# Keys transposed in blocks on VectorE, wider products for values and wo: 1186 TensorE instructions instead of 2224

## The chip, the core and the metric

The kernel runs on one core of a Trainium2 chip. The core has TensorE (matrix products into PSUM), VectorE, ScalarE and GpSimd (elementwise work), and SyncE, which here issues nearly all transfers. All transfers run over 16 DMA engines. In the profile the engines are called PE (PEld for its weight loads), DVE, ACT, POOL and SP. The metric is the device time of one execution in microseconds (us), the median of several runs.

## What is computed

A decode step for one token: an attention block and a gated feed-forward block side by side, both fed by the same layer norm of `x`, and their sum added to `x`. All data are float32.

```python
xn = _layernorm(x)                                # x: 1 x 1 x 1024
# attention: 32 query heads, 4 key/value heads of 128, last W = 4096 of 65536 positions
q = xn @ wq                                       # 1024 x 4096
k, v = k_cache[:, :, Sk - W:, :], v_cache[:, :, Sk - W:, :]   # each repeated for 8 query heads
p = softmax(q . k * Dh ** -0.5)
attention = (p @ v).reshape(1, 1, 4096) @ wo      # 4096 x 1024
# feed-forward
h = gelu_tanh(xn @ w_gate) * (xn @ w_up)          # each 1024 x 3584
out = x + attention + h @ w_down                  # 3584 x 1024
```

Each weight and each key and value of the window is used once: 94.4 MB are read and 4 KB written.

## The kernel before

**Stream.** One tile, `ring` (128 partitions x 32768 floats), holds whatever is being read. The list `PLAN` gives the loads in order, each with its column and the load whose place it takes: wq in two halves (q0, q1), then keys and values of heads 0 and 1 (k0, v0), w_gate's first half (g0), keys and values of heads 2 and 3 (k1, v1), w_gate's second half (g1), w_up's first half in two quarters (ua, ub) and its second half (u1), wo in two halves (o0, o1), a small piece of w_down (m), and w_down in three parts (d0, d1, d2). After a load has been worked on, `used` issues the loads that take its place, on SyncE's queue in that order. So o0 waits for the last reader of ua and ub, o1 for u1, d0 for o0, d1 and d2 for o1.

**Order.** The loop at lines 774 to 824 walks `PLAN` and emits the work on each load. Every engine does its instructions in the order in which they are emitted. The class `Flow` notes which tile columns each instruction touches and, in a second pass, puts in the waits between engines and for transfers; PSUM is tracked by whole banks. Nearly every instruction goes through one helper, so the profile puts them all on line 225, and tiles tell them apart.

**Projections** (`project`, lines 468 to 482). A load of wq, w_gate or w_up holds four rows per partition (the input index is 512 jj + 4 p + r). Rows r = 0 and 2 go to TensorE: `xz` holds the normalized input in one column of 32 zeroed ones, and the 512-wide blocks of the weights run through four 32-column strips of the array into the PSUM tile `acc`. Rows 1 and 3 go to VectorE, which adds weight times input into the SBUF tile `part`; `projected` then sums `part` over the partitions on TensorE into the same `acc`.

**Attention.** `transpose_keys` (511 to 522) turns a head's 4096 x 128 keys with 32 TensorE transposes into PSUM and copies them out in eight 512-wide pieces on ScalarE and VectorE; `scores` runs the queries against each piece, and VectorE takes maxima; `exponentials` are ScalarE's. `transpose_probs` turns the probabilities through TensorE; `values` (563 to 575) multiplies each 32-partition strip with its own 128 columns of values. After the values of heads 2 and 3, `maxima` (582 to 590) is emitted, with its VectorE part, ahead of the work on g1; `factors` and `normalizers` follow later, and `heads` scales the outputs after ub.

**Feed-forward.** `gelu` and `gated` work on `acc` for w_gate and w_up as 128 x 512 and 96 x 512. `hidden` (664 to 698) brings the hidden vector onto the partitions with 32 small TensorE products and copies into `hz`.

**Output.** `outputs` splits wo's 32 rows per partition: even ones go to TensorE, `accumulate` with four 256-wide products each, odd ones to VectorE into `out_part`. `downs` does the same for w_down; the last pieces of d2 are narrow, so that little work is left behind the last transfer. Of d2, 32 pieces of 3 KB are loaded as ten small transfers into `moved` instead, which changes how many bytes each of the 16 DMA engines gets.

Of the kernel before, what the change touches and what calls it, by code (L numbers as in the profile page):

```python
# [25 lines left out]
DOWN = (16, 8, 4)  # L26
PIECES = ((0, 16), (0, 4, 8), (0, 2, 3, 4))
KEPT = (1, 3, 5, 7, 9, 11)
EPS = 1e-5
# [5 lines left out]
MC = 768  # L35
MOVED = ((0, 0, 0, 12, 4), (0, 1, 12, 12, 4), (1, 0, 24, 5, 1), (1, 1, 29, 3, 1))
SIZES = {"tp": NB, "acc": 2 * NB, "part": 8 * NB, "rows": 2 * NB}
# [16 lines left out]
class Flow:  # L54
# [4 lines left out]
    def __init__(self, nc, plan=None):  # L59
# [3 lines left out]
        self.touched = {}  # L63
        self.sems = {}
# [44 lines left out]
    def note(self, k, ins):  # L109
# [3 lines left out]
        for access, writes in [(a, False) for a in ins.ins] + [(a, True) for a in ins.outs]:  # L113
# [22 lines left out]
            self.touched[name] = kept  # L136
        self.ops.append((engine, dma, needs))
# [128 lines left out]
def decode_layer(nc, x, k_cache, v_cache, wq, wo, w_gate, w_up, w_down, out):  # L266
# [16 lines left out]
    def source(kind, i):  # L283
# [11 lines left out]
        return grouped(w_down, P * sum(DOWN[:i]), DOWN[i])  # L295
# [4 lines left out]
    def load(key, at):  # L300
# [18 lines left out]
        if key == ("d", 2):  # L319
            end = 2 * n - MC  # L320
            nc.gpsimd.memset(loaded[key][:, end:2 * n], 0.0)
            both = src[:, 0:2].rearrange("p t n -> p (t n)")
            nc.sync.dma_start(loaded[key][0:P:2, :2 * n], both[0:P:2])
            nc.sync.dma_start(loaded[key][1:P:4, :2 * n], both[1:P:4])
            nc.sync.dma_start(loaded[key][3:P:4, :end], both[3:P:4, :end])
            pieces = pieces[1:]
# [4 lines left out]

    moved = consts.tile([P, 2, MC], F32, name="moved")
    moved_h = consts.tile([P, 2], F32, name="moved_h")

    def load_moved():


        rest = w_down[DF - 4 * P:, D - MC:].rearrange("(r x) n -> x r n", x=16)[13]
        for s, a, first, count, step in MOVED:
            for j in range(step):  # L340
                to = 32 * a + j
                nc.sync.dma_start(
                    moved[to:to + 4 * (count // step):4, s], rest[first + j:first + count:step]
                )
# [8 lines left out]
    x_rows = work.tile([NJ, NR * P], F32, name="x_rows")  # L353
# [3 lines left out]
    x_out = work.tile([P, CO], F32, name="x_out")  # L357
    nc.vector.memset(x_out, 0.0)
# [6 lines left out]
    ident = consts.tile([P, P], F32, name="ident")  # L365
    nc.gpsimd.memset(ident, 0.0)
# [7 lines left out]
    xz = consts.tile([P, NR, NJ, 32], F32, name="xz")  # L374
    nc.vector.memset(xz, 0.0)
    qz = consts.tile([P, 2, 32], F32, name="qz")
    nc.vector.memset(qz, 0.0)

    hz = consts.tile([P, TD + 1, 32], F32, name="hz")
    nc.vector.memset(hz, 0.0)  # L380
    nc.gpsimd.memset(moved, 0.0)
    nc.gpsimd.memset(moved_h, 0.0)
    oz = consts.tile([P, HQ + 1, 32], F32, name="oz")
    nc.vector.memset(oz, 0.0)
    units = consts.tile([P, 2, 32], F32, name="units")
    nc.vector.memset(units, 0.0)
    nc.vector.memset(units[:, 0, 31:32], 1.0)
    unit = units.rearrange("p t m -> p (t m)")[:, 31:63]

    same = consts.tile([P, 4, 32], F32, name="same")  # L390
    nc.vector.tensor_add(same[:, 0, :], ident[:, 0:32], ident[:, 32:64])
    nc.vector.tensor_add(same[:, 1, :], ident[:, 64:96], ident[:, 96:128])
# [20 lines left out]
    def layer_norm():  # L413
        xt_p = small("xt_p")
        for r in range(NR):
# [29 lines left out]
            xz[:, :, :, 0], xc.rearrange("p (r j) -> p r j", r=NR), st[:, 7:8], None, op0=ALU.mult  # L445
# [14 lines left out]
    def blocks(kind, z, w, count, start, stop):  # L460
        for n in range(count):
            b, c = divmod(n, 4)
            nc.tensor.matmul(
                acc[kind][32 * c:32 * c + 32, b, :], z, w[:, n * NB:(n + 1) * NB],
                start=start, stop=stop,
            )

    def project(kind, jj, w, rows, count):
        n = count * NB
        for k, r in enumerate(rows):  # L470
            first = jj == 0 and r < 2
            if first and r == 0:
                acc[kind] = psum.tile([P, 2, NB], F32, name="acc_" + kind, tag="acc")
                part[kind] = work.tile([P, 8 * NB], F32, name="part", tag="part")
# [6 lines left out]
    def projected(kind, count):  # L481
        blocks(kind, unit, part[kind], count, False, True)
# [6 lines left out]
    def queries(q_sb):  # L489
        q_p = psum.tile([P, 2, 4, 4], F32, name="q_p", tag="tp", bufs=2)  # L490
        for b in range(2):
            for hh in range(4):
                nc.tensor.matmul(
                    q_p[:, b, hh, :], q_sb[:, b, hh * P:(hh + 1) * P], ident[:, 0:P:32],
                    start=True, stop=True,
                )
            nc.vector.tensor_copy(
                qz[:, b, 0:16].rearrange("p (s t h) -> p s t h", s=2, t=2),
                q_p[:, b].rearrange("p h (s t) -> p s t h", s=2),
            )  # L500
# [10 lines left out]
    def transpose_keys(g, kn, steps, vector):  # L511
        if g not in keys:
            keys[g] = work.tile([P, 8, NB], F32, name="kT")
# [260 lines left out]
    for key, _, _ in PLAN:  # L774
# [33 lines left out]
        elif kind in ("ua", "ub", "u"):  # L808
# [4 lines left out]
            elif kind == "ub":  # L813
                heads()
# [36 lines left out]
```

## Time and profile before

| | |
|---|---|
| time, median of 3 runs | 226.21 us (226.15 to 226.31) |
| profiled execution, first to last instruction | 224.8 us |
| TensorE matmuls busy | 126.0 us, 1107 instructions, and as many weight loads |
| VectorE busy | 112.1 us |
| ScalarE busy | 28.2 us |
| GpSimd busy | 2.8 us |
| read from memory | 94.38 MB, 420 GB/s over the span |
| instruction packets on queue 8 | 8, 0.13 MB |

The span is the time from the first to the last instruction of one profiled execution; that execution has no other time of its own, and the runs' median lies 1.4 us above the span. A row of the timeline reads: start, duration, engine, line, operation, output tile <- input tiles, shape, how many instructions were merged, and in brackets the idle time before it and what ended that. A transfer appears with the engine that issued it (SPq), and the row shows the issue, not the transfer; when it has landed can be read from the first instruction that waited for it.

### The profile page before, as it was taken

Reading aid. Unit: us, or ns where it says so; the run is one execution under the profiler, and the core shown is the slowest. Engines: PE = TensorE matmul, PEld = TensorE weight load, DVE = VectorE, ACT = ScalarE, POOL = GpSimd, SP = SyncE. Lnnn points to the kernel's source line nnn. Section 1 sums busy time; section 2 is a strip of 40 time slices with the busy share of each in tenths; the row PEclk is TensorE's granted clock in tenths of the full one; section 3 lists DMA queues with packets and bytes.
Section 4 is the critical chain, followed back from the end, with each engine's and each line's share of the span. In section 5 each row is a group of like instructions: output and inputs, shape, how many; then the busy total and the mean of one; then the engine's idle time right before and its main releaser. Section 6 shows DMA issues by size and latency. Waiting matters only on the chain.

```text
span 224.8 us, 2511 instructions
## 1 busy us (share of the span) xinstructions
PE 126.0 (56%) x1107; PEld 65.6 (29%) x1107; DVE 112.1 (50%) x142; ACT 28.2 (13%) x54; POOL 2.8 (1%) x9
## 2 busy tenths in 40 slices
PE   0120910539899891999836751237308988900976
PEld 0010200104634731755601110001003887400442
DVE  7030920591333282336039489339708932992942
ACT  2030000002415600454400220000000000000000
POOL 3000000000000000000000000000000000010000
PEclk9999975596969999799988795557965855665699
DMA  9889889799997999999989999999989989999994
GB/s 374 374 385 548 373 373 560 338 408 464 439 490 338 429 443 452 391 488 408 472 355 449 434 449 429 490 399 420 469 385 455 467 385 461 434 397 394 426 407 172
DMA packets 3194, 94.53 MB, mean 421 GB/s; under 512 B 446, under 2 KB 718, under 8 KB 1040
## 3 DMA queue, kind: packets, MB, share of 16 engines
q1 hardware_dynamic: 3160, 94.38, 97.8%
q8 instruction: 8, 0.13, 0.2%
q14 instruction: 2, 0.02, 0.0%
q10 hardware_dynamic: 24, 0.01, 0.0%
HBM read 94.38 MB, written 0.00 MB: 420 GB/s over the span
## 4 chain that ended last, share of the span: by engine, by line
DMA 67%; DVE 20%; PE 10%; SPq 1%; ACT 1%; issue 1%; POOL 0%; DVEq 0%
DMA ring<-in_B_w_gate 26%; DMA ring<-in_A_wq 18%; DMA ring<-in_A_wo 13%; DVE part L225 13%; DMA ring<-in_B_w_down 10%; PE tp L225 6%; PE out L225 3%; DVE out_part L225 3%; DVE rows L225 2%; SPq L225 1%; PE acc L225 1%; DVE g_sb L225 1%; ACT kT L225 1%; DVE hz L225 1%; DVE kT L225 0%
## 5 line engine op out<-in xcount | busy, mean ns | idle before, releaser
L225 PE MATMUL acc<-ring,xz 128*32 128x512 f32 x176 | 32.2, 808 | 37.3 <-DMA ring<-in_A_wq 22.2
L225 DVE SCALAR_TENSOR_TENSOR part<-ring,xz,part 128x3584 f32<-128x3584 f32 (+1 forms) x9 | 37.2, 4129 | 22.0 <-DMA ring<-in_A_wq 12.5
L225 PE MATMUL tp<-ident,ring 128*128 128x128 f32 x128 | 21.0, 309 | 7.1 <-DMA ring<-in_A_k_cache 5.0
L225 PEld LDWEIGHTS acc<-ring,xz 128*32 128x32 f32 x176 | 7.2, 139 | 58.2 <-issue 26.7
L225 DVE SCALAR_TENSOR_TENSOR out_part<-ring,oz,out_part 128x1024 f32<-128x1024 f32 x16 | 20.6, 1285 | 0.6
L225 PEld LDWEIGHTS tp<-ident,ring 128*128 128x128 f32 x128 | 15.4, 154 | 16.7 <-DMA ring<-in_A_k_cache 5.9
L225 PE MATMUL out<-ring,hz 128*32 128x256 f32 x168 | 12.1, 438 | 13.5 <-DMA ring<-in_B_w_down 13.4
L225 DVE COPY kT<-tp 128x512 f32<-128x512 f32 x12 | 8.1, 690 | 19.1 <-PE tp L225 19.1
L225 PE MATMUL out<-ring,oz 128*32 128x256 f32 x120 | 12.0, 586 | 9.6 <-DMA ring<-in_A_wo 9.6
L225 ACT ACTIVATE kT<-tp 128x512 f32<-128x512 f32 x20 | 11.5, 596 | 26.6 <-PE tp L225 26.6
L225 PE MATMUL tp<-ident,kT 128*128 128x4 f32 (+4 forms) x64 | 13.4, 343 | 1.6 <-DVE hz L225 1.6
L225 PEld LDWEIGHTS tp<-ident,kT 128*128 128x128 f32 (+2 forms) x64 | 13.1, 294 | 2.2 <-DVE hz L225 1.8
L225 PE MATMUL acc<-part,units 128*32 128x512 f32 x44 | 8.1, 817 | 8.7 <-DVE part L225 8.7
L225 DVE TENSOR_SCALAR part<-ring,xz 128x3584 f32<-128x3584 f32 (+1 forms) x3 | 6.5, 2171 | 12.3 <-DMA ring<-in_A_wq 7.5
L225 PEld LDWEIGHTS out<-ring,hz 128*32 128x32 f32 x168 | 5.6, 125 | 20.0 <-DMA ring<-in_B_w_down 15.8
L225 PEld LDWEIGHTS out<-ring,oz 128*32 128x32 f32 x120 | 5.7, 166 | 16.0 <-DMA ring<-in_A_wo 10.6
L225 DVE SCALAR_TENSOR_TENSOR out_part<-ring,hz,out_part 128x1024 f32<-128x1024 f32 x6 | 7.7, 1285 | 4.9 <-DMA ring<-in_B_w_down 4.7
L225 PE MATMUL s<-kT,qz 128*32 128x512 f32 x64 | 9.3, 709 | 0.0
L225 DVE TENSOR_REDUCE m<-s 128x2 f32<-128x1024 f32 x4 | 4.9, 1225 | 7.7 <-PE s L225 7.7
L225 PE MATMUL o<-ring,pT 128*32 128x128 f32 x256 | 7.8, 274 | 1.0 <-ACT pT L225 1.0
L225 PEld LDWEIGHTS o<-ring,pT 128*32 128x32 f32 x256 | 6.7, 110 | 1.9 <-ACT pT L225 1.9
L225 PE MATMUL tp<-ident,x_rows 2*128 2x2 f32 x4 | 0.6, 253 | 10.4 <-DMA x_rows<-in_A_x 10.4
(96 smaller groups left out, 73.3 us busy)
## 6 DMA issues: line engine op xcount, KB each, us to landing
ring<-in_B_w_gate SPq DMA_DIRECT2D x2, 7168.0 KB, 29.5
ring<-in_A_k_cache SPq DMA_DIRECT2D x4, 2048.0 KB, 19.0
ring<-in_A_v_cache SPq DMA_DIRECT2D x2, 4096.0 KB, 26.1
ring<-in_B_w_up SPq DMA_DIRECT2D x2, 3584.0 KB, 22.3
ring<-in_B_w_up SPq DMA_DIRECT2D x1, 7168.0 KB, 25.8
ring<-in_B_w_down SPq DMA_DIRECT2D x2, 2048.0 KB, 20.7
ring<-in_B_w_down SPq DMA_DIRECT2D x2, 512.0 KB, 21.1
ring<-in_B_w_down SPq DMA_DIRECT2D x2, 256.0 KB, 21.2
```

Of the source, the lines that this page charges most:

```text
L225: return lambda *a, **k: self.flow.issue(self.engine, lambda: call(*a, **k))
```

## The change

Loads, their order and their places in `ring` stay the same, but for w_down's tail.

- **Keys.** `turn_keys` transposes a head's keys where they lie, in 32 x 32 blocks, with one VectorE instruction of 128 x 4096. `spread_keys` then copies the sixteen (partition group, block column) combinations, 32 partitions x 1024 elements each, to their places in a second tile: four on GpSimd, seven on VectorE, five on ScalarE. The tile has two buffers. The work is emitted as turn, spread, turn (next head), scores, spread (next head), exponentials, scores.
- **Values.** Two strips at a time: 64 partitions x 256 columns, half of which `heads` uses, so that `heads` has eight scaled additions instead of four.
- **Projections.** The dictionary `VECTOR` says which rows go to VectorE: six of wq's eight, five of w_gate's, seven of w_up's (before, four of each). TensorE's blocks of w_gate and w_up are 512 and 384 wide, eight of them.
- **GELU** is fused into three VectorE instructions per half. `hidden` transposes with two VectorE instructions.
- **wo and w_down.** `accumulate_halves` takes a row in two 512-wide products, alternately on the lower and the upper two strips; `add_halves` adds its four sums into `out_part`. Three more rows of wo go to VectorE.
- **Tail of w_down.** Every fourth partition's first three rows of d2 (12 KB each, 32 of them, with one dummy row before them whose factor is zero) are left out of d2 and loaded into `moved` by three transfers of eleven rows.
- Zeroed tiles become one tile and one memset; a few constants are added; GpSimd's instructions wait for the one before.

```diff
+LONG, SHORT = 16, 12
+WIDTHS = (NB, P // 4 * SHORT)
+WO_KEPT = ((14,), (2, 6, 14))
+PAIRED = 18
+VECTOR = {
+    ("q", 0): (0, 1, 2, 3), ("q", 1): (1, 3), ("g", 0): (1, 2, 3), ("g", 1): (1, 3),
+    ("u", 0): (0, 1, 2, 3), ("u", 1): (1, 2, 3),
+}
...
+OWN = 11
+AWAY = 3
...
+        if engine == ENG.Pool and not dma:
+            needs.update(self.pool)
+            self.pool = [k]
...
         if key == ("d", 2):
...
+            nc.gpsimd.memset(loaded[key][:, :AWAY * n], 0.0)
+            for t, end in zip(pieces, pieces[1:3]):
+                part_of = src[:, t:end].rearrange("p t n -> p (t n)")
+                for some in (slice(0, P, 2), slice(1, P, 4)):
+                    nc.sync.dma_start(loaded[key][some, t * n:end * n], part_of[some])
+            pieces = pieces[2:]
...
+        moved.append(work.tile([P, AWAY, D], F32, name="moved", tag="part"))
+        there = moved[0][:32 + 4 * OWN].rearrange("p t n -> p (t n)")
+        nc.gpsimd.memset(there, 0.0)
...
+        for j in range(3):
+            nc.sync.dma_start(
+                there[32 + j:32 + 4 * OWN:4],
+                rest[OWN * j:OWN * j + OWN, at * D:(at + AWAY) * D],
+            )
...
-            if r % 2 == 0:
-                blocks(kind, xz[:, r, jj, :], wr, count, first, False)
+            if r not in VECTOR[kind, jj]:
...
+                blocks(kind, xz[:, r, jj, :], wr, first, False)
             else:
-                add_scaled(part[kind][:, :n], wr, xz[:, r, jj, 0:1], first)
...
+                add_scaled(part[kind][:, :n], wr, xz[:, r, jj, 31:32], first)
...
-    def transpose_keys(g, kn, steps, vector):
...
+    def turn_keys(kn):
+        nc.vector.transpose(kn, kn)
+
+    def spread_keys(g, kn):
+        keys[g] = work.tile([P, 8, NB], F32, name="kT", bufs=2)
+        kT = keys[g].rearrange("p i n -> p (i n)").rearrange("p (j a k) -> p j a k", a=4, k=32)
+        kn = kn.rearrange("p (j b k) -> p j b k", b=4, k=32)
+        for n in range(16):
+            a, b = n % 4, (n + n // 4) % 4
+            to, of = kT[32 * b:32 * b + 32, :, a], kn[32 * a:32 * a + 32, :, b]
+            if a == b:
+                nc.gpsimd.tensor_copy(to, of)
+            elif n % 2 or n == 4:
+                nc.vector.tensor_copy(to, of)
             else:
-                nc.scalar.activation(keys[g][:, i, :], t_p, AF.Copy)
+                nc.scalar.activation(to, of, AF.Copy)
...
-                for c in range(4):
-                    j = 16 * b + 4 * c + jj
+                for c in (0, 2):
                     nc.tensor.matmul(
-                        o_p[32 * c:32 * c + 32, g, :], pT[:, b, jj, 32 * c:32 * c + 32],
-                        vn[:, j * DH:(j + 1) * DH],
-                        start=(b == 0 and jj == 0), stop=(b == 1 and jj == 3),
+                        o_p[32 * c:32 * c + 64, g], pT[:, b, jj, 32 * c:32 * c + 64],
+                        vn[:, b, c:c + 2, jj], start=(b == 0 and jj == 0), stop=(b == 1 and jj == 3),
                     )
...
         for g in range(2):
...
+            for n in range(4):
+                f, t = divmod(n, 2)
+                add_scaled(
+                    o_sb[:, g, :], o_p[:, 2 * g + f, t], weights[:, g, f, t:t + 1], n == 0
+                )
...
+        for b, n in enumerate(WIDTHS):
+            gs, ts, hs = g_sb[:, b, :n], t_sb[:, b, :n], h_sb[:, b, :n]
+            nc.scalar.activation(gs, acc["g"][:, b, :n], AF.Copy)
+            nc.vector.scalar_tensor_tensor(ts, gs, 0.044715, gs, op0=ALU.mult, op1=ALU.mult)
+            nc.vector.scalar_tensor_tensor(ts, ts, 1.0, gs, op0=ALU.add, op1=ALU.mult)
             nc.scalar.activation(hs, ts, AF.Tanh, scale=GELU_C)
+            nc.vector.scalar_tensor_tensor(gs, hs, 1.0, gs, op0=ALU.add, op1=ALU.mult)
...
+        t = 0
+        for b, count in enumerate((LONG, SHORT)):
+            rows = h_sb[:, b, :32 * count].rearrange("p (k t) -> p t k", t=count)
+            nc.vector.transpose(hz[:, t:t + count, :], rows)
+            t += count
...
+    def accumulate_halves(z, w, stop=False):
...
+        a = len(halves) % 2
+        for b in range(2):
+            c = 2 * a + b
+            nc.tensor.matmul(
+                half_p[32 * c:32 * c + 32], z, w[:, b * NB:(b + 1) * NB],
+                start=len(halves) < 2, stop=stop,
+            )
+        halves.append(a)
+
+    def add_halves():
+        for c in range(4):
+            r, cols = slice(32 * c, 32 * c + 32), slice(c % 2 * NB, c % 2 * NB + NB)
+            nc.vector.tensor_add(out_part[r, cols], out_part[r, cols], half_p[r])
...
-            transpose_keys(2 * i, kn[:, :half], range(8), (1, 4, 6))
+            turn_keys(kn[:, :half])
             if i == 0:
                 queries(q_sb)
+            spread_keys(2 * i, kn[:, :half])
+            turn_keys(kn[:, half:])
             s = scores(2 * i)
-            transpose_keys(2 * i + 1, kn[:, half:], range(4), ())
+            spread_keys(2 * i + 1, kn[:, half:])
             exponentials(2 * i, s)
-            transpose_keys(2 * i + 1, kn[:, half:], range(4, 8), (4, 5, 7))
             s = scores(2 * i + 1)
```

More of the change, by code (lines that the diff above doesn't have):

```diff
@@ L356, in decode_layer @@
         nc.scalar.dma_start(x_rows[j:j + 1, :], x_in[j:j + 1, :])
-    x_out = work.tile([P, CO], F32, name="x_out")
-    nc.vector.memset(x_out, 0.0)
+    sizes = (CO, NR * NJ * 32, 2 * 32, (TD + 1) * 32, (HQ + 1) * 32, 2 * 32)
+    zeros = consts.tile([P, sum(sizes)], F32, name="zeros")
+    nc.vector.memset(zeros, 0.0)
+    ends = [sum(sizes[:k]) for k in range(len(sizes) + 1)]
+    x_out, xz, qz, hz, oz, units = (zeros[:, a:b] for a, b in zip(ends, ends[1:]))
+    xz = xz.rearrange("p (r j m) -> p r j m", j=NJ, m=32)
+    qz, hz, oz, units = (z.rearrange("p (t m) -> p t m", m=32) for z in (qz, hz, oz, units))
     x_in = x.rearrange("a b (h c n) -> (a b c) h n", h=2, c=4)
@@ L588, in maxima @@
         )
-        for c in range(1, 4):
-            nc.vector.tensor_copy(top[:, c, :], top[:, 0, :])
+        nc.vector.tensor_copy(top[:, 1:4, :], top[:, 0:1, :].to_broadcast([2, 3, 32]))
     def factors():
@@ L653, in gelu @@
             nc.scalar.activation(hs, ts, AF.Tanh, scale=GELU_C)
-            nc.vector.tensor_scalar(hs, hs, 0.5, 0.5, op0=ALU.mult, op1=ALU.add)
-            nc.vector.tensor_mul(gs, gs, hs)
+            nc.vector.scalar_tensor_tensor(gs, hs, 1.0, gs, op0=ALU.add, op1=ALU.mult)
     def gated():
-        for b in range(2):
-            n = rows[b]
-            h = copies[b][:n]
-            g, u = (a.unsqueeze(1).to_broadcast(h.shape) for a in (g_sb[:n, b], acc["u"][:n, b]))
-            nc.vector.tensor_mul(h, g, u)
@@ L694, in hidden @@
[L694 to L702 removed]
+                h_p[r, :AWAY], where[:, 4 * a:4 * b], hz[:, t:t + AWAY, 31], start=True, stop=True
+            )
+            nc.vector.tensor_copy(moved_h[r], h_p[r, :AWAY])
@@ L736, in downs @@
         tiles = [loaded["d", i][:, n * D:(n + 1) * D] for i in range(3) for n in range(DOWN[i])]
[L737 to L738 removed]
+        n = 32 + 4 * OWN
+        for s in range(AWAY):
+            add_scaled(out_part[:n], moved[0][:n, s], moved_h[:n, s:s + 1], False)
         for t in KEPT:
```

210 lines of the change are left out of this document (81 added, 129 removed).

## The prediction

> **What bounds the kernel now.** I read the busy shares first, then the queues, then the chain that ended last.
>
> ```profile
> span 224.8 us, 2511 instructions
> PE 126.0 (56%) x1107; PEld 65.6 (29%) x1107; DVE 112.1 (50%) x142; ACT 28.2 (13%) x54; POOL 2.8 (1%) x9
> q1 hardware_dynamic: 3160, 94.38, 97.8%
> q8 instruction: 8, 0.13, 0.2%
> DMA 67%; DVE 20%; PE 10%; SPq 1%; ACT 1%; issue 1%; POOL 0%; DVEq 0%
> ```
>
> The 16 DMA engines are full: SP's queue alone takes 97.8% of their time, VectorE only half of its own. The chain nevertheless holds 20% VectorE, because a load may start only when the ring columns under it are read. So the question for any edit is whether each load is still issued before the queue runs dry. If so, VectorE and TensorE time costs nothing; if not, each us late is a us lost. The stretch where that is closest runs from the second half of w_gate to wo:
>
> ```profile
> 116.11 7.94 DVE L225 SCALAR_TENSOR_TENSOR part<-ring,xz,part 128x3584 f32<-128x3584 f32 x2 [3.48 <-DMA ring<-in_B_w_gate]
> 124.10 3.31 PE L225 MATMUL acc<-part,units 128*32 128x512 f32 x14 [2.50 <-DVE part L225]
> 126.10 0.60 ACT L225 ACTIVATE g_sb<-acc 128x512 f32<-128x512 f32 x1 [1.75 <-PE acc L225]
> 134.00 2.08 DVE L225 TENSOR_SCALAR part<-ring,xz 128x3584 f32<-128x3584 f32 x1
> 136.46 3.95 DVE L225 SCALAR_TENSOR_TENSOR part<-ring,xz,part 128x3584 f32<-128x3584 f32 x1
> 140.43 17.78 SPq L225 DMA_DIRECT2D ring<-in_A_wo  x2
> 149.92 7.94 DVE L225 SCALAR_TENSOR_TENSOR part<-ring,xz,part 128x3584 f32<-128x3584 f32 x2 [5.87 <-DMA ring<-in_B_w_up]
> 169.46 0.75 DVE L225 TENSOR_SCALAR out_part<-ring,oz 128x1024 f32<-128x1024 f32 x1 [7.00 <-DMA ring<-in_A_wo]
> ```
>
> wo's first half is issued at 140.43, as the product over ub ends (136.46 + 3.95). Up's second half is seen landed at 149.92, wo's first half at 169.46: 19.54 us for 8.39 MB at the full rate. The queue would run dry about 149.9, so this issue has some 9.5 us in hand, less the time a transfer needs to start. The first load of all started on an empty queue:
>
> ```profile
> 0.73 0.89 SPq L225 DMA_DIRECT2D ring<-in_A_wq  x2
> 22.64 2.35 DVE L225 TENSOR_SCALAR part<-ring,xz 128x4096 f32<-128x4096 f32 x1 [7.46 <-DMA ring<-in_A_wq]
> 25.02 4.48 DVE L225 SCALAR_TENSOR_TENSOR part<-ring,xz,part 128x4096 f32<-128x4096 f32 x1
> ```
>
> Its 8.39 MB took 22.64 - 0.73 = 21.9 us, so starting cold costs 0 to 2.4 us beyond the 19.5; I take 1.4, as part of the 2.4 is launch. The room at wo is then about 8.1 us.
>
> **The keys.** The change takes 32 TensorE transposes and eight PSUM copies per head away and gives VectorE two kinds of work. *Transposes in place*, 4096 columns: not shown before; bounds 2.35 us (one source, row at 22.64) and 4.48 (row at 25.02). I take 4.45: 32x32 blocks have to be filled and emptied, so I expect one element per cycle. *Spread copies*, 16 per head of 32 partitions x 1024 elements, 7 on VectorE, 5 on ScalarE, 4 on GpSimd. VectorE's nearest row is the 0.75 for 1024 at 169.46, which also loads a factor; the 2.35 row scaled to 1024 gives 0.59; a two-source product of 1024 takes 1.285. I take 0.70, so 4.9 per head (4.1 to 9.0).
>
> ```profile
> 53.94 1.02 ACT L225 ACTIVATE rows<-acc 128x1024 f32<-128x1024 f32 x1 [38.49 <-PE acc L225]
> 1.24 1.38 POOL L225 MEMSET moved<- 128x1536 f32 x1
> L225 DVE SCALAR_TENSOR_TENSOR out_part<-ring,oz,out_part 128x1024 f32<-128x1024 f32 x16 | 20.6, 1285 | 0.6
> ```
>
> ScalarE's five take 5 x 1.02 = 5.1 and GpSimd's four, by the memset, at least 4 x 0.92 = 3.7, beside VectorE's and the next transpose. Keys 0 and 1 have room:
>
> ```profile
> 51.00 0.33 SPq L225 DMA_DIRECT2D ring<-in_B_w_gate  x1
> 59.86 1.05 PE L225 MATMUL tp<-ident,rows 128*128 128x4 f32 x8
> 71.07 1.12 SPq L225 DMA_DIRECT2D ring<-in_A_k_cache  x2
> ```
>
> VectorE is free at 51.0, as w_gate's load goes out; 4.45 + 1.7 (two query transposes of 1.05, partly under the first key transpose) + 4.9 + 4.45 + 1.8 (scores' maximum, below) + 4.9 frees the first keys' columns at 73.2, 2.1 later than 71.07, while w_gate's first half is seen landed only at 79.56.
>
> **Keys 2 and 3, where it bites.** All VectorE work here is in order.
>
> ```profile
> 79.56 2.08 DVE L225 TENSOR_SCALAR part<-ring,xz 128x3584 f32<-128x3584 f32 x1 [4.80 <-DMA ring<-in_B_w_gate]
> 81.68 3.95 DVE L225 SCALAR_TENSOR_TENSOR part<-ring,xz,part 128x3584 f32<-128x3584 f32 x1
> 89.29 4.19 PE L225 MATMUL tp<-ident,ring 128*128 128x128 f32 x20 [4.96 <-DMA ring<-in_A_k_cache]
> 102.80 1.92 PE L225 MATMUL s<-kT,qz 128*32 128x512 f32 x16
> 104.80 1.22 DVE L225 TENSOR_REDUCE m<-s 128x2 f32<-128x1024 f32 x1 [1.19 <-PE s L225]
> 106.63 0.75 ACT L225 ACTIVATE p<-s,bias 128x512 f32<-128x512 f32 x1 [0.20 <-DVE bias L225]
> 108.19 1.09 PE L225 MATMUL tp<-ident,p 128*128 128x128 f32 x8 [0.24 <-ACT p L225]
> 109.53 1.95 PE L225 MATMUL o<-ring,pT 128*32 128x128 f32 x64 [0.25 <-ACT pT L225]
> 111.84 0.41 DVE L225 TENSOR_REDUCE top<-tp 2x32 f32<-2x256 f32 x1 [5.24 <-PE tp L225]
> ```
>
> Three rows of w_gate's first half instead of two: 79.56 + 2.08 + 3.95 + 3.95 and gaps = 89.65; the keys are there (89.29). Then transpose 4.45, copies 4.9, transpose 4.45, maximum and bias of the scores 1.8 (104.80 to just before 106.63), copies 4.9: the keys are ready at 110.15. Scores cannot now begin after the first blocks, since each copy writes into all column groups; they take 2.0, up to the maximum.
>
> *Wider values.* 64 products of 128 columns and 32 partitions took 1.95; now 32 of 256 columns and 64 partitions. Four 32-wide strips fill the array; if two 64-wide ones run at a time, the same per-column pace gives 32 x 2 x 1.95/64 x 2 = 3.9; if four still overlap 1.95; if one by one 7.8. I take 3.9, nothing being saved by fewer instructions that stream longer. The Trainium skill, "TensorEngine Tiling (Array Packing)", section "Performance Considerations", speaks the same way against the change: a stationary side of at most 32 columns allows fourfold column tiling, one of 64 only twofold. By it the values cost the 3.9 taken here; no row before has a 64-wide strip to test it.
>
> From 110.15: scores 2.0; transposes of head 2's probabilities until a first half is copied 1.35 (108.19 to 109.53); values 3.9; the same for head 3 1.35 and 3.9; maxima through TensorE and VectorE 0.9 (111.48, where the values ended, to 112.25 and a copy). That is 13.4, hence 123.5. The exponentials (106.63 and 108.19 bound them: 1.55) end meanwhile. VectorE's maxima stand in its queue ahead of the second half of w_gate, so that starts at 123.5, not 116.11: 7.4 late.
>
> **From there to wo's issue.** Products over w_gate 7.94, as before. Sums to PSUM 2.0 until ScalarE may copy (124.10 to 126.10). GELU:
>
> ```profile
> 126.73 0.69 DVE L225 TENSOR_TENSOR rows<-g_sb 128x512 f32<-128x512 f32 x1 [2.11 <-ACT g_sb L225]
> 128.65 0.63 ACT L225 ACTIVATE kT<-rows 128x512 f32<-128x512 f32 x1 [1.95 <-DVE rows L225]
> ```
>
> Before it lasted 126.10 to 134.00, 7.9. Fused, its first half is 0.60 + 2 x 0.69 + 0.63 + 0.69 and gaps = 3.4, its 384-wide second 2.25: 5.65, saving 2.25. But all four rows of up's first half are VectorE's, not two: 2.08 + 3 x 3.95 and gaps = 14.0 instead of 6.05, so 7.95 more; a weights product adds 0.2. Net 5.9 more. So wo's issue moves 7.4 + 5.9 = 13.3, to 153.7. Of this 8.1 lies in the room computed above; 5.2 is idle DMA. Up's own issues (VectorE done with w_gate at 131.5) fall at the edge of their room and stay inside this delay.
>
> **What is hidden or small.** wq's first half wholly on VectorE: 2.35 + 3 x 4.48 = 15.8 from 22.64, ready at 38.4 while the second half still lands. The first key half's columns are free at 29.5. After wo's issue, everything hangs on the same late transfer: heads 5.1 (3.7 before, rows below, and four products of 0.35 more), three w_up rows 11.9, so wo's second issue comes by 170.7, some 4 us before the first half is through (153.7 + 1.4 + 19.5); three more wo rows (3 x 1.285) lie under wo's second half; the later memset (128 x 3072, 2.8 by the POOL row) ends well ahead of the last w_down load. The transposes of the hidden vector on VectorE instead of TensorE (7.10 for its first 32 products) shorten a stretch nobody waits for; w_down's last columns still arrive last.
>
> ```profile
> 140.32 0.35 DVE L225 TENSOR_SCALAR o_sb<-o,weight 128x128 f32<-128x128 f32 x1
> 143.47 0.58 DVE L225 TENSOR_REDUCE oz<-rows 128x32 f32<-128x256 f32 x1
> 175.21 7.10 PE L225 MATMUL tp<-ident,kT 128*128 128x4 f32 x32
> ```
>
> *A gain on the queue itself.* Eight 16 KB instruction packets held 0.2% x 224.8 x 16 = 7.2 us of engine time, 0.9 each. At 1186 instead of 2224 TensorE instructions I expect four or five: about 0.2 us saved on average, up to 0.9 on an engine that had one. The 33 rows shift 12 KB onto engines 0 to 10 and 24 KB off the other five (each engine had two 12 KB rows of the 32 left out; three come back to eleven engines). At 94.38 MB / 16 over 219.9 us (97.8% of the span), 12 KB is 0.46 us. If the remaining fetches are on those five, both together win some 0.5. After a pause that restarts all engines together, I credit 0.4.
>
> **The sum** for the profiled execution: 224.8 + 5.2 - 0.4 = 229.6; the median 226.21 lies 1.4 above the span, so **231.0 us**.
>
> **The rivals.**
>
> *A: starvation before wo, as summed, 228.5 to 233.5.* For: VectorE's order and the nine rows above. Against: two prices, transpose and values, are bounds.
>
> *B: the loads stay covered, and it is faster.* Place: VectorE between 89.65 and 116. It decides if w_gate's second half starts no more than 8.1 - 5.9 = 2.2 us late. That happens with the transposes at the 2.35 row (two save 4.2) and values at four strips at a time (two save 3.9): 8.1 off 7.4. Then only the queue's gain is left: 226.2 - 0.5 = 225.7. Against: both extremes are wanted at once, or one of them and the copies at 0.59 (14 save 1.5) with a transfer that starts in no time (1.4).
>
> *C: a little starvation*, one of the two extremes: 231.0 - 4.0 = 227.0, 226.7 to 228.5 with the copies; within 0.2% only when the rest cancels the queue's gain.
>
> *D: the copies collide.* GpSimd's and VectorE's copies taking turns add 3.7 per head, twice on the path: 231.0 + 7.4 = 238.4; one element per cycle (1.285) adds 14 x 0.58 = 8.1. No row before has GpSimd copying beside VectorE. The Trainium skill, "GPSIMD Engine Reference", section "Key points", says that GpSimd shares its SBUF interfaces with VectorE and contends with two-port VectorE instructions, which the fast copies would be; it would give this 238.
>
> **How the numbers follow.** A 0.48, B 0.23, C 0.15, D 0.14. Range 225.3 to 235.5: B and C inside, most of A, D's lower part; about 0.15 left out. A's own range is 228.5 to 233.5. What a measurement of this kernel can tell from no change is 0.2%, 0.45 us. Faster: B's 0.23 and a little of C, 0.24; same 0.08 (B's and C's edges); slower 0.68.
>
> **What would show it.** Right: the DMA slices fall below 9 between about 150 and 156 us; wo's issue near 153.7, up's second half landed some us earlier; w_gate's second products begin near 123.5; transposes near 4.45; values near 3.9; copies near 0.70. Wrong: w_gate's second products still at 116 to 118 and a DMA share near 97%: then B. Copies above 1.2 or gaps between them beside POOL: then D.

## The result and the profile after

The changed kernel takes 244.99 us (median; 243.34 to 245.71), the kernel before, beside it, 226.19: 1.082 times as long (95% interval 1.078 to 1.086), 18.8 us more. Forecast were 231.0 us and a range from 225.3 to 235.5. The direction was right, the size was not, and the time lies outside the range. An execution more than 1.5% above the fastest of its kernel is left out of the ratios below, but not of the medians; that concerns one of the old keys (230.35 us) and one of the old values (243.91 us).

The page of the kernel after: span and instructions, busy shares, the DMA slices (one digit for each 6.1 us), the two queues, and the shares of the chain that ended last.

```profile
span 244.1 us, 1506 instructions
PE 85.7 (35%) x587; PEld 31.9 (13%) x587; DVE 181.2 (74%) x164; ACT 37.7 (15%) x54; POOL 27.4 (11%) x26
DMA  9899998999989868999893899939798989999990
q1 hardware_dynamic: 3098, 94.39, 91.3%
q8 instruction: 4, 0.07, 0.1%
DVE 46%; DMA 36%; PE 12%; issue 3%; ACT 2%; SPq 0%; DVEq 0%
```

The DMA engines are no longer full: 91.3% instead of 97.8%. VectorE holds 46% of the chain instead of 20%. The slices fall to 6 and 8 near 85 to 95 us, to 3 near 130 and to 3 near 160. TensorE's busy time fell by 40 us and brought nothing (587 products and as many weight loads in this profile, 1174, against 2214 before; the title's 1186 and 2224 stand in no profile).

The timeline of the kernel after, from the first half of w_gate to the landing of wo's first half:

```profile
82.90 2.08 DVE L237 TENSOR_SCALAR part<-ring,zeros 128x3584 f32<-128x3584 f32 x1
92.87 4.44 DVE L237 STREAM_TRANSPOSE ring<-ring 128x4096 f32<-128x4096 f32 x1
97.34 7.86 DVE L237 COPY kT<-ring 32x1024 f32<-32x1024 f32 x7
97.37 5.89 POOL L237 COPY kT<-ring 32x1024 f32<-32x1024 f32 x4 [23.38 <-DVE ring L237]
105.23 4.45 DVE L237 STREAM_TRANSPOSE ring<-ring 128x4096 f32<-128x4096 f32 x1
105.26 3.64 PE L237 MATMUL s<-kT,zeros 128*32 128x512 f32 x16 [12.14 <-DVE kT L237]
111.21 0.69 DVE L237 SCALAR_TENSOR_TENSOR bias<-m,away 128x2 f32<-128x2 f32 x1
111.93 6.37 DVE L237 COPY kT<-ring 32x1024 f32<-32x1024 f32 x7
118.45 3.64 PE L237 MATMUL s<-kT,zeros 128*32 128x512 f32 x16 [9.55 <-DVE kT L237]
123.82 3.67 PE L237 MATMUL o<-ring,pT 128*64 128x256 f32 x32
128.77 3.67 PE L237 MATMUL o<-ring,pT 128*64 128x256 f32 x32 [0.25 <-ACT pT L237]
132.79 0.41 DVE L237 TENSOR_REDUCE top<-tp 2x32 f32<-2x256 f32 x1 [8.84 <-PE tp L237]
133.41 7.92 DVE L237 SCALAR_TENSOR_TENSOR part<-ring,zeros,part 128x3584 f32<-128x3584 f32 x2
155.59 7.93 DVE L237 SCALAR_TENSOR_TENSOR part<-ring,zeros,part 128x3584 f32<-128x3584 f32 x2
163.55 17.35 SPq L237 DMA_DIRECT2D ring<-in_A_wo  x2
185.46 1.63 DVE L237 TENSOR_SCALAR p<-ring,zeros 128x1024 f32<-128x1024 f32 x1 [1.00 <-DMA ring<-in_A_wo]
```

It is the predicted chain, longer at four places: w_gate's first products start late, both groups of VectorE copies take longer, and so do the scores. The pause near 130 us lies in front of w_up's second quarter, issued at 132.47; VectorE doesn't wait for that load (it works from 148.94 to 163.5 without a wait for data). Wo is issued at 163.55 instead of 140.43 and seen landed at 185.46 instead of 169.46: 16.0 of the span's 19.3 us are lost by then. The other 3.3 are lost behind it.

### The profile page after: what moved, and what is told of

The parts are those of the page before. It is cut to its first block, busy times and chain, and to the rows that moved or that the text cites. A ratio compares the mean times of both kernels' runs of the same rounds, so it can differ in the third digit from the quotient of the medians.

```text
span 244.1 us, 1506 instructions
## 1 busy us (share of the span) xinstructions
PE 85.7 (35%) x587; PEld 31.9 (13%) x587; DVE 181.2 (74%) x164; ACT 37.7 (15%) x54; POOL 27.4 (11%) x26
## 3 DMA queue, kind: packets, MB, share of 16 engines
q1 hardware_dynamic: 3098, 94.39, 91.3%
## 4 chain that ended last, share of the span: by engine, by line
DVE 46%; DMA 36%; PE 12%; issue 3%; ACT 2%; SPq 0%; DVEq 0%
DVE part L237 20%; DMA ring<-in_A_wq 17%; DVE kT L237 11%; DMA ring<-in_A_wo 10%; DMA ring<-in_B_w_down 10%; DVE ring L237 5%; PE o L237 5%; DVE p L237 4%; PE s L237 3%; PE acc L237 2%; DVE m L237 2%; PE tp L237 2%; DVE rows L237 1%; ACT pT L237 1%; DVE bias L237 1%
## 5 line engine op out<-in xcount | busy, mean ns | idle before, releaser
L237 DVE SCALAR_TENSOR_TENSOR part<-ring,zeros,part 128x3584 f32<-128x3584 f32 (+1 forms) x15 | 61.9, 4127 | 3.8 <-DMA ring<-in_A_wq 3.4
L237 DVE SCALAR_TENSOR_TENSOR p<-ring,zeros,p 128x1024 f32<-128x1024 f32 x25 | 32.1, 1285 | 7.6 <-DMA ring<-in_A_wo 4.5
L237 POOL COPY kT<-ring 32x1024 f32<-32x1024 f32 x16 | 20.9, 1309 | 92.2 <-DVE ring L237 91.5
L237 PE MATMUL s<-kT,zeros 128*32 128x512 f32 x64 | 14.6, 1060 | 38.9 <-DVE kT L237 38.9
L237 DVE COPY kT<-ring 32x1024 f32<-32x1024 f32 x28 | 27.7, 988 | 0.4
L237 ACT ACTIVATE kT<-ring 32x1024 f32<-32x1024 f32 x20 | 21.1, 1053 | 24.3 <-DVE ring L237 24.1
L237 PE MATMUL s<-ring,zeros 128*32 128x512 f32 x96 | 16.7, 817 | 22.4 <-DMA ring<-in_B_w_down 16.0
L237 PE MATMUL acc<-ring,zeros 128*32 128x512 f32 (+2 forms) x104 | 13.5, 656 | 28.5 <-DMA ring<-in_A_wq 28.5
L237 DVE STREAM_TRANSPOSE ring<-ring 128x4096 f32<-128x4096 f32 x4 | 17.8, 4443 | 0.7 <-DMA ring<-in_A_k_cache 0.6
L237 PE MATMUL o<-ring,pT 128*64 128x256 f32 x128 | 14.7, 382 | 0.7 <-ACT pT L237 0.5
L237 ACT ACTIVATE rows<-acc 128x1024 f32<-128x1024 f32 x1 | 1.0, 1024 | 38.9 <-PE acc L237 38.9
```

What stands on the lines that cost most here:

```text
L237: return lambda *a, **k: self.flow.issue(self.engine, lambda: call(*a, **k))
```

## The experiments

The theory (V): the loads wait for VectorE's in-order chain from w_gate's first half to wo's issue, and what each changed part puts on that chain is what it costs, once the room of some 8 us is used up. The rivals: the seven rows more on VectorE are the loss (S); the keys alone are (K); the new end costs by itself (E); TensorE's clock is the cause. In the table the time is the median, and wo's issue is read in one profiled execution, which is not always the median one: with the old keys that one took 226.88 us, with the old shares 235.5, with the old values 243.91, and with the moved rows cut in nines 228.14.

| kernel | issue of wo, us | time, us | against before (95%) |
|---|---|---|---|
| before | 140.43 | 226.2 | 1 |
| after | 163.55 | 244.99 | 1.078 to 1.086 |
| after, old keys | 145.68 | 227.77 | 1.004 to 1.008 |
| after, old shares | 152.37 | 237.85 | 1.041 to 1.056 |
| after, old values | 160.37 | 242.43 | 1.057 to 1.076 |
| after, GpSimd copies nothing | 160.99 | 243.34 | 1.074 to 1.081 |
| after, TensorE kept busy | 162.21 | 243.47 | 1.073 to 1.081 |
| after, maxima later | 157.83 | 240.64 | 1.058 to 1.066 |
| after, old shares and values | 149.55 | 235.26 | 1.038 to 1.042 |
| after, old keys, shares and values | 138.07 | 226.99 | 1.002 to 1.005 |
| the same, moved rows cut in nines | 137.57 | 226.86 | 1.002 to 1.006 |
| the same, no moved rows | 138.46 | 226.48 | 1.000 to 1.002 |
| block transposes, the rest of the chain undone | 142.17 | 230.87 | 1.019 to 1.027 |
| old keys, fewer shares, no moved rows | 142.03 | 226.39 | 1.000 to 1.002 |

**The old keys.**

```diff
-            turn_keys(kn[:, :half])
...
-            spread_keys(2 * i, kn[:, :half])
+            transpose_keys(2 * i, kn[:, :half], range(8), (1, 4, 6))
```

> The changed kernel, but the keys go through TensorE and PSUM as before (no block transposes, no spread copies); shares of VectorE, wide values and the rest stay. Theory V (VectorE's in-order chain from the first half of w_gate to the issue of wo sets the end): w_gate's first products start when their data land (79.6 us, not 82.9), the last keys are ready near 103.7 as before, the wide values (3.67 us each, not 1.95) put the maxima at about 116, wo's issue follows 30.1 later at 146, the queue hardly runs dry: 226 to 228 us. Rival S (the seven rows more on VectorE are the main loss, the keys little): about 236 to 240. Rival E (the rearranged end, with its later last additions, costs some us by itself): 229 or more.

Measured 227.77 us: theory V, and 17.2 of the 18.8 us are gone with this part alone. The timeline of the kernel with the old keys:

```profile
79.44 2.09 DVE L237 TENSOR_SCALAR part<-ring,zeros 128x3584 f32<-128x3584 f32 x1 [8.44 <-DMA ring<-in_B_w_gate]
115.97 7.94 DVE L237 SCALAR_TENSOR_TENSOR part<-ring,zeros,part 128x3584 f32<-128x3584 f32 x2 [0.20 <-DMA ring<-in_B_w_gate]
145.68 17.35 SPq L237 DMA_DIRECT2D ring<-in_A_wo  x2
```

Both halves of w_gate are worked on as they land, and wo's issue at 145.68 just keeps the queue full (wo's first half is seen landed at 169.29, before at 169.46), with all seven further rows and the wide values still there. Rival S falls.

**The old shares.**

```diff
-VECTOR = {
-    ("q", 0): (0, 1, 2, 3), ("q", 1): (1, 3), ("g", 0): (1, 2, 3), ("g", 1): (1, 3),
-    ("u", 0): (0, 1, 2, 3), ("u", 1): (1, 2, 3),
-}
+VECTOR = {(k, j): (1, 3) for k in "qgu" for j in range(2)}
```

> The changed kernel, but VectorE takes rows 1 and 3 of every load, as before; keys, values and the rest stay as changed. Theory V: two rows fewer in w_up's first half take 7.95 us out of the chain to wo's issue, one row fewer of w_gate only about 1.2, because then the second keys' landing (91.2 us) is waited for: wo's issue at about 154.4 instead of 163.55, 236 us in all. Rival K (the keys alone make the loss, these rows lie beside it): 244 to 245, wo's issue unmoved. Rival S: 228 or less.

Measured 237.85, 7.1 us less than the changed kernel (1.9 more than expected), with wo's issue at 152.37. Theory V again, against K. But with the old keys the same rows cost next to nothing: the price of the shares exists only because the keys have used up the room.

**The old values.**

```diff
-                for c in (0, 2):
+                for c in range(4):
```

> The changed kernel, but the values go 32 partitions x 128 columns at a time as before. Theory V: both values of heads 2 and 3 stand in the chain in front of the maxima, 3.67 against 1.95 us each, so wo's issue comes 3.4 us earlier and the time is 241 to 242. If 64-wide strips run as fast per useful column as 32-wide ones, and the 3.67 is a low clock alone, the old form would take as long: 244 to 245.

Measured 242.43 (239.89 to 243.91), 2.6 us less, with wo's issue 3.2 us earlier: as the chain has it, within a wide interval. In the place of the 3.67 us the narrow products took 1.96, here for head 2:

```profile
124.06 1.96 PE L237 MATMUL o<-ring,pT 128*32 128x128 f32 x64 [0.23 <-ACT pT L237]
```

That the 64-wide strips themselves are slow, and not the clock, the next rows show as well.

**The clock and the strips.** In the changed kernel a second look: the windows around the scores and the values (busy time of PE, PEld, DVE, ACT, POOL, then granted clock, DMA share, GB/s).

```profile
105.00:109.00 4.00, 3.64 (x16) 0.60 (x16) 3.97 (x2) 0.00 (x0) 0.00 (x0) 0.50 1.06 459
122.00:132.00 10.00, 9.63 (x82) 6.71 (x80) 1.70 (x4) 3.64 (x8) 0.00 (x0) 0.94 0.66 280
```

The scores run at half clock, right after TensorE has waited 12 us for the keys; the values at 0.94, so their 3.67 against 1.95 is the strips. To test the first, products that nobody reads were added while the copies go on:

```diff
+    def warm(g, kn):
+        w_p = small("w_p")
+        for k in range(18):
+            c = k % 4
+            nc.tensor.matmul(
+                w_p[32 * c:32 * c + 32], qz[:, g // 2, :], kn[:, k % 8 * NB:k % 8 * NB + NB],
+                start=True, stop=True,
+            )
```

> The changed kernel with 18 products added per head whose results nobody reads: TensorE runs the transposed keys as they lie against the queries while the spread copies go on. If the scores' 3.64 us instead of 1.92 is the granted clock (0.50 in that window, after TensorE has stood idle), they take about 1.9 again, and head 3's probabilities' transposes 1.1 instead of 1.7: 1.7 to 2.3 us less in front of the maxima, 1.7 less in front of w_gate's first products, so 241 to 242. If the copies' layout makes the scores slow, they stay at 3.64 and the time at 244 to 246.

```profile
104.42 1.92 PE L237 MATMUL s<-kT,zeros 128*32 128x512 f32 x16 [1.38 <-DVE kT L237]
117.62 3.60 PE L237 MATMUL s<-kT,zeros 128*32 128x512 f32 x16 [4.23 <-DVE kT L237]
```

The scores of heads 1 and 2 took 1.92 us each, at a granted clock of 1.00 (104.4 to 106.4 us). Those of head 3 stayed at 3.60, at 0.53 (117.6 to 121.2 us), since TensorE ran out of products 4.23 us ahead of them. So the clock is the cause of the slow scores, but the gain is smaller than expected: 243.47 us, 1.5 less, with intervals that overlap.

**No copies on GpSimd.**

```diff
-            if a == b:
-                nc.gpsimd.tensor_copy(to, of)
-            elif n % 2 or n == 4:
+            if n % 2 or n == 4:
```

> The changed kernel, but GpSimd copies nothing: two of its four copies per head go to VectorE (nine in all), two to ScalarE (seven). If GpSimd's copying slows VectorE's (rows of 1.43 us beside it, 0.69 without): every VectorE copy takes about 0.69 us, nine 6.2 us, ScalarE's seven 7.4 end last, each head is ready 0.5 to 1.2 us earlier, three us in all on the chain: about 242. If the 1.43 has another cause (quadrants, strides): copies stay at 0.99 on average, nine take 8.9, and the time grows to 247 or more.

The groups of copies (minimum, median and maximum in ns), first in the kernel with the old shares, where GpSimd copies, then without:

```profile
L234 DVE COPY kT<-ring x28: 681/689/1439, 57.1 to 114.9; 32x1024 f32<-32x1024 f32 x28
L234 POOL COPY kT<-ring x16: 1030/1383/1565, 56.3 to 110.9; 32x1024 f32<-32x1024 f32 x16
```

```profile
L237 DVE COPY kT<-ring x36: 681/686/690, 56.4 to 114.7; 32x1024 f32<-32x1024 f32 x36
L237 ACT ACTIVATE kT<-ring x28: 1052/1053/1057, 56.2 to 113.2; 32x1024 f32<-32x1024 f32 x28
```

Without GpSimd none of 36 copies on VectorE takes more than 0.69 us; beside it some take 1.44. Contention is shown. Yet the kernel gains only 1.65 us (243.34), half of what was expected, with intervals that overlap: ScalarE, with seven copies of 1.05 us in front of its exponentials, now ends last (7.45 us of copies for head 2, against 6.28 for VectorE's nine).

**The maxima later.**

```diff
-            if i == 1:
-                maxima()
...
             if i == 1:
+                maxima()
                 state = factors()
```

> The changed kernel with one thing moved: the maxima's part on VectorE and TensorE is emitted behind w_gate's second products, not ahead of them. Theory V with the queue order as a part of the loss: VectorE, idle from 123.95 to 132.8, starts those products at about 124 instead of 133.4; the maxima (0.9 us) follow later; wo's issue comes some 8 us earlier, at 155 to 156: 236 to 238 us. If the values themselves (not the order) hold that work, through PSUM or TensorE: 244 to 245.

```profile
123.99 7.93 DVE L237 SCALAR_TENSOR_TENSOR part<-ring,zeros,part 128x3584 f32<-128x3584 f32 x2
135.63 0.41 DVE L237 TENSOR_REDUCE top<-tp 2x32 f32<-2x256 f32 x1 [3.70 <-PE tp L237]
```

The products start at 123.99, as expected, so the order was a part of the loss. But the maxima then wait until 135.63, 3.70 us with VectorE idle, since TensorE has w_gate's products in front of their transposes. Wo's issue comes 5.7 us earlier, not 8, and the time is 240.64 instead of 236 to 238.

**The keys as the only part on the chain.** Old shares and old values together (the two diffs above).

> The changed kernel with VectorE's shares and the values as before: of the three parts on the chain only the keys are left changed. Theory V: from the run with the old shares alone (wo's issue at 152.4, 237.9 us) the narrower values take another 3.4 us off: wo's issue at 149, 234 us. Rival (parts overlap, the values count only beside the shares): 237 to 238.

Measured 235.26, 1 us over V's sum, far from the rival. The keys alone cost 8.3 us (against 226.99 without them), and 17.2 with the other two parts present: past the room, the parts add up within about 1 us.

What pays for the late chain is not wo's issue alone, though. Here wo is issued at 149.55, but w_up's second half, which before was seen landed at 149.92, is seen only at 156.14:

```profile
156.14 7.94 DVE L234 SCALAR_TENSOR_TENSOR part<-ring,zeros,part 128x3584 f32<-128x3584 f32 x2 [2.96 <-DMA ring<-in_B_w_up]
```

So 6.2 of the 8.8 us by which this span (233.6) exceeds the one before are lost at the loads in front of wo: the second keys go out at 77.59 instead of 71.07, w_gate's second half at 91.44 instead of 85.66, w_up at 115.88 instead of 101.35. The column of wo's issue says how late the chain is, not by itself how much time is lost.

**The rest.** Keys, shares and values all as before.

> The changed kernel with keys, values and VectorE's shares all as before: left are the fused GELU, the hidden vector's transposes on VectorE, the two-product rows of wo and w_down, three more wo rows on VectorE, the 33 rows of 12 KB and the constants. Theory V: nothing is on the chain to wo's issue, which comes near 138; some 1700 to 1800 TensorE instructions leave six packets or so; 225.7 to 226.3. Rival E (the new end costs): 227.0 or more, with the last additions on VectorE and TensorE at a low clock behind the last transfer.

Measured 226.99: wo's issue at 138.07 has room, and still the kernel is 0.3% slower than before. Theory V's 225.7 to 226.3 is missed. Rival E holds for this remainder, 0.8 us of the 18.8. Two changes of the moved rows were tried, first two rows of each fourth partition in four transfers of nine, nine, nine and six instead of three rows in three transfers of eleven, then none:

```diff
-OWN = 11
-AWAY = 3
+OWN = 9
+AWAY = 2
```

> The run with keys, values and shares as before, and w_down's moved rows cut otherwise: two rows of each fourth partition (8 KB) instead of three, by four transfers of nine, nine, nine and six, so that they lie on engines 0 to 8. If that run's 0.8 us over the kernel before is two of its seven instruction packets on engines that also carry 12 KB more (w_down's first part ended at 209.0 us there, 207.7 before), this one ends it near 207.6 and takes 225.7 to 226.3, level with the kernel before or a little better. If the loss is the end itself (TensorE's products behind the last 16 KB rows, 4.5 us one after the other), it stays at 226.8 to 227.1.

```diff
-        if key == ("d", 2):
-            nc.gpsimd.memset(loaded[key][:, :AWAY * n], 0.0)
...
-            pieces = pieces[2:]
```

> The run with keys, values and shares as before (226.99 us), with no rows of w_down moved at all: d2 is loaded whole, the small transfers, their memset and their additions are gone. If the 33 rows are what makes w_down's second part land 1.3 us later than before (218.8 against 217.5), it now lands at about 217, TensorE's work behind it starts 1.5 us earlier and the time is 226.0 to 226.4. If the rows do not matter and the cost is the work behind the last pieces, 226.8 to 227.2.

The cut in nines gave 226.86, no change; no moved rows gave 226.48, just over what was expected and 0.13% over the kernel before. What a reader can see of it is when TensorE may start on w_down's second part, here the 32 products on its last four rows, first in the kernel before, then with the 33 rows, then without moved rows:

```profile
217.98 1.93 PE L225 MATMUL out<-ring,hz 128*32 128x256 f32 x32 [1.25 <-DMA ring<-in_B_w_down]
```

```profile
219.36 1.93 PE L234 MATMUL o<-ring,zeros 128*32 128x256 f32 x32 [1.88 <-DMA ring<-in_B_w_down]
```

```profile
218.10 1.93 PE L234 MATMUL o<-ring,zeros 128*32 128x256 f32 x32 [1.68 <-DMA ring<-in_B_w_down]
```

With the 33 rows the last of these rows land 1.3 to 1.4 us later. So the rows cost about 0.5 us in this kernel, together with what goes with them and was left out too: memsets, small products and three additions of 76 x 1024 on VectorE. Which of these it is was not tested, and why the cut in nines didn't help stays open.

**Block transposes with the rest of the chain undone**: old shares and values, nothing on GpSimd, maxima later.

> Block transposes kept, everything else that the runs found on VectorE's chain undone: values and shares as before, GpSimd copies nothing, maxima behind w_gate's second products. Theory V adds the parts up: from the run with the keys alone (wo's issue at 149.6) 1.5 to 2 us less for the copies and 5 to 6 for the maxima put it at 142 to 143, ahead of the end of w_up's last load: the pause before wo is gone, what is left are pauses of 1 us each before the second keys and w_up: 227.5 to 229. If block transposes cost by themselves, beside the chain (SBUF traffic, a slower queue): 231 or more.

Wo's issue came at 142.17 as expected, and the DMA share of this run's page is 97.0%, near the 97.8 before. The time, 230.87, is 2 to 3 us over the expectation, though, and its interval reaches past the 231 us from which the rival, block transposes that cost by themselves, would hold. The loss lies ahead of wo: w_up's second half is seen landed at 153.12 instead of 149.92, 3.2 of the 3.8 us by which this span exceeds the one before. The queue pauses for about 1 us before the values of heads 2 and 3 (88 us) and more shortly before both quarters of w_up (113 and 115 us). Two stretches of this kernel, then the nearest two of the kernel before; the last number of a row is GB/s:

```profile
96.00:112.00 16.00, 3.64 (x16) 0.68 (x16) 15.13 (x19) 12.54 (x12) 0.00 (x0) 0.61 1.02 442
115.50:126.00 10.50, 10.01 (x176) 6.54 (x172) 8.52 (x6) 3.72 (x8) 0.00 (x0) 0.83 0.97 369
```

```profile
96.00:112.00 16.00, 14.31 (x210) 9.34 (x202) 5.55 (x12) 8.17 (x18) 0.00 (x0) 1.00 1.05 451
116.00:126.00 10.00, 7.38 (x40) 1.93 (x43) 8.21 (x5) 0.21 (x1) 0.00 (x0) 0.71 1.01 436
```

While the block transposes and copies run (96 to 112 us) the queue moves nearly what it moved before, 442 GB/s against 451. It is slow behind the pauses, 369 against 436, when no transpose or copy runs any more. That speaks for the late issues and against the transposes' own traffic, but it was not tested apart.

**Fewer instructions where there is room**: old keys, wide values, no moved rows, VectorE's shares raised for wq's first half (all four rows) and both halves of w_up (rows 1 to 3).

> Keys as before, wide values, no moved rows, and VectorE's shares raised only where the chain has room: all of wq's first half, rows 1 to 3 of both w_up halves, rows 1 and 3 of w_gate. Theory V: wo's issue near 142, ahead of the 146.5 from which it costs; five or six instruction packets instead of eight: 226.0 to 226.5. If the wide values or the shares cost anything beside that chain: 227.5 or more.

Measured 226.39 us, 1.0008 of before (0.9999 to 1.0017): the same time with 1486 TensorE instructions instead of 2214 in the profile (743 products and as many weight loads, against 1107). Taking TensorE instructions away is free where VectorE has the room. No run beat the kernel before.

## Why the prediction was right and wrong

**The mechanism held.** The forecast's stretch from the second half of w_gate to wo's issue was 30.2 us; it took 163.55 - 133.41 = 30.1, and its parts fit one by one. The transposes were priced at 4.45 and took 4.45. The fused GELU was put at 5.65 and took it. Values at 3.9 took 3.67, against 1.95 for the narrow ones, at an almost full clock (0.94). The Trainium skill, "TensorEngine Tiling (Array Packing)", section "Performance Considerations", allows 64 columns only twofold tiling; these rows agree.

**What failed are two prices, met twice, in front of that stretch, and two terms behind.** The copies and the scores were priced too low. Wo's issue was forecast at 153.7 and came at 163.55, 9.85 later:

- *"Keys 0 and 1 have room"*: 3.2 us. That step stopped where the first keys' columns are free, at 73.2. VectorE's queue goes on in order: head 1's scores and their maximum now stand in front of w_gate's first products. At the forecast's own prices this would have been harmless, since 73.2 + 2.0 + 1.8 is 77.0, and w_gate is seen landed at 79.56. With the copies and scores as they were, w_gate's products started at 82.90, 5.9 us after 77.0, and only 2.6 of that was room:

```profile
56.84 7.40 DVE L237 COPY kT<-ring 32x1024 f32<-32x1024 f32 x7
70.96 6.37 DVE L237 COPY kT<-ring 32x1024 f32<-32x1024 f32 x7
77.48 3.64 PE L237 MATMUL s<-kT,zeros 128*32 128x512 f32 x16 [9.55 <-DVE kT L237]
81.18 1.23 DVE L237 TENSOR_REDUCE m<-s 128x2 f32<-128x1024 f32 x1 [3.84 <-PE s L237]
```

The transpose for head 2 began at 92.87 and not 89.65. These 3.2 us are no third cause, but the next two terms met one stage earlier.
- *The copies at 4.9 us per head*: for heads 2 and 3 they took 7.86 and 6.37 with a 0.69 us bias in front, in all 25.45 us from the transpose at 92.87 to the keys ready, not 20.5: 4.95 us. This was rival D, put at 0.14, and its cause is shown: GpSimd's copies beside VectorE's. Where they overlap a copy of 0.69 takes 1.44, and even a 128 x 2 instruction took 0.69 instead of 0.16. The Trainium skill, "GPSIMD Engine Reference", section "Key points", named the contention; by its rule the price came out as 238 us, and its direction is what the runs show. The contention should have stood in the sum, since the copies of both engines were known to run side by side.
- *Scores at 2.0 us*: they took 3.64. With the first transposes of probabilities at 1.68 instead of 1.09 and the values a little shorter, the way from the keys to the end of the maxima took 15.1 us and not 13.4: 1.7. The row they were priced by, 1.92, came from a place with key transposes right ahead. With these gone, TensorE idles for 9 to 12 us and its granted clock is 0.50. The Trainium skill states this, "TensorE: Matmul & The Clock Gate", section "What's actually happening": half the clock after one idle window of about 3.4 us. The traces agree (0.50 at the scores; 1.92 us again with TensorE kept busy; 3.60 behind 4.23 us without products). The kernel before has the other price too, and the forecast did not use it as a bound: head 0's scores, behind 16 products of only four columns, took 3.56 us at a clock of 0.57 (62 to 66 us):

```profile
62.17 3.56 PE L225 MATMUL s<-kT,qz 128*32 128x512 f32 x16
```

The step failed by moving a duration to a place with another clock.

3.2 + 4.95 + 1.7 is 9.85, the whole error of the issue. Behind it:

- *A cold start of 1.4 us*: wo's first half took 185.46 - 163.55 = 21.9 us, the full 2.4 over 19.5, as the very first load did. 1.0 us.
- *"w_down's last columns still arrive last" and 0.4 us credited to the queue*: from wo's landing to the end the kernel took 58.6 us, not 55.3 less 0.4. 3.7 us; by the rows, 1.3 until w_down's first part is seen (40.0 us behind wo instead of 38.7, with the 33 rows in between) and 2.0 behind that, of which 1.15 passes until its last four rows are seen; why is not shown.

The page after, its end:

```profile
225.46 7.13 PE L237 MATMUL s<-ring,zeros 128*32 128x512 f32 x48 [16.01 <-DMA ring<-in_B_w_down]
236.41 3.35 PE L237 MATMUL o<-ring,zeros 128*32 128x256 f32 x32 [2.96 <-DMA ring<-in_B_w_down]
240.02 1.47 PE L237 MATMUL o<-ring,zeros 128*32 128x256 f32 x24
```

The same 32 products took 1.93 us before, at a granted clock of 1.00 (215 to 220 us), and 3.35 here, at 0.58 (236 to 240 us). TensorE runs from 236.41 on without waiting for data, so the end hangs on it and no longer on the last transfer.

The terms give 231.0 + 9.85 + 1.0 + 3.7 = 245.55 us; the profiled execution took 245.51. That they close is bookkeeping, since each is a measured time less its forecast; the causes rest on the experiments.

**The rivals.** B and C wanted a faster transpose or four strips at a time; both are excluded by rows. D was right in kind: by its own sign, copies above 1.2 us beside GpSimd, it came true beside A, with 4.4 of its 7.4 us. None of the four contained a low clock or the late start, so the range's upper end, 235.5, was too near: the bounds of unknown durations were taken only from rows with TensorE warm and VectorE alone.

## What to carry to other kernels

A duration belongs to the place it was measured in: before moving a row to a new place, ask whether the engine is still warm there and who shares its path to memory. When an engine is given work, walk its whole queue in order from the first place that gets later, not only the load that is nearest to its limit; here the two wrong prices cost 3.2 us in a stage that the forecast had left, besides the one that it added up. Taking work off an engine that nobody waits for buys nothing by itself. On the engine that receives it the work costs time once the loads' room is used up, while inside the room it is free (226.39 us with a third fewer TensorE instructions).

## What the runs showed of the hardware

- Copies of 32 x 1024 floats: 0.69 us on VectorE alone, up to 1.44 beside GpSimd, whose own take 1.38 to 1.55 while VectorE copies all the while (head 2) and 1.03 at the least. Where they overlap, both lose.
- A transfer on an empty queue takes 2.4 us longer to land for 8.39 MB, in the middle of a kernel as at its start (21.9 against 19.5 us). A pause costs more than its length.
- Block transposes and copies of 32 x 1024 hardly slow the DMA queue: 442 GB/s while they run, against 451 in the same stretch (96 to 112 us) of the kernel before.
